# A start tile's load in halves on two queues with an earlier turning, and bn_stats of the up weights in three slots instead of two

## The chip, the cores and the metric

The kernel runs on one core of a Trainium2 chip. The metric is the device time in microseconds (us) of that core, as the median of several executions. Engines are written as in the profile: PE is the matmul engine and PEld its weight loads, DVE the vector engine, ACT the scalar engine, POOL the general-purpose engine, SP the sync engine. SPq and ACTq are the sequencers of SP and ACT, and they issue the loads. A load is issued when its sequencer hands it to the DMA engines, and it has landed when all its data have arrived.

## The reference

```python
def _A_ref(x, wqkv, w_phi, wo):          # x: 1 x 2048 x 512, H = 32 heads of 16
    q, k, v = (x @ wqkv) split into heads
    pq, pk = q @ w_phi, k @ w_phi        # per head
    phi_q = concat(softmax(pq), softmax(-pq));  phi_k likewise
    kv = phi_k^T v;  z = sum over s of phi_k
    return (phi_q kv / (phi_q z + 1e-6)) @ wo

def _B_ref(x, w_gate, w_up, w_down):     # F = 1792
    return ((x @ w_gate) * (x @ w_up)) @ w_down

xn = layernorm(x)
return x + _A_ref(xn, ...) + _B_ref(xn, ...)
```

Everything is bf16. (The code above is condensed from the reference; `setup_inputs` is left out.)

## The kernel before

A small scheduler in the kernel records each instruction with what it reads and writes, and places it on its engine. Between `sc.pin = True` and `sc.pin = False` the order of recording is kept. The parts that matter here are these.

The loads of the start. A tile of x is 128 tokens of 512 numbers, 128 KB; a slice of the v weights is 128 KB too. `SP` and `ACT` name the engine whose sequencer issues the load; SP is the default.

```python
    sc.pin = True
    load_x(0, 1)
    load_x(1, 1, ACT)
    load_v(SP, 0)
    load_v(ACT, 1)
    load_x(2, 1)
    load_v(ACT, 3)
    load_v(SP, 2)
    load_x(3, 1)
    load_gu(SP, 0, (1,))          # first slice of the up weights, 256 KB
    act(sbf("lnv", 0, 1), eps_f, ["eps"], ["pace"])
    load_gu(ACT, 0, (0,))         # first slice of the gate weights, 256 KB
    # ... (later loads cut)
```

The centring of a tile: ACT sums one half of the columns, DVE the other, then DVE subtracts the mean.

```python
    def ln_mean_split(t):
        act(xn_tile(t)[:, 256:], x_tile(t)[:, 256:], [("x", t)], [("mu", t)], scale=1.0 / 512.0,
            accum=mu[:, t:t + 1])
        dve(lambda e: e.tensor_scalar(out=xn_tile(t)[:, :256], in0=x_tile(t)[:, :256], scalar1=1.0 / 512.0,
                                      scalar2=0.0, op0=ALU.mult, op1=ALU.add, accum_out=mua[:, t:t + 1]),
            [("x", t)], [("mua", t)], 256)
```

The pinned start. `warm` is a matmul of constants, `x_transpose` turns half a tile on PE (2 transposes) and copies it back on ACT or DVE, `v_matmul(t, b, qs)` multiplies tile t with the v weights qs.

```python
    warm(7)
    warm(1, 512, [("x", 0)])
    sc.pin = True
    ln_mean_split(0)
    ln_mean_split(1)
    # ... (centring of tiles 0 and 1, turning of tile 0 and of half of tile 1 cut)
    ln_mean_split(2)
    x_transpose(1, 5, 1, DVE)
    warm(1, 128)
    ln_center_whole(2)
    for t in range(2):
        v_matmul(t, t, ((0, 1),), stop=False)
    for t in range(2):
        v_matmul(t, t, ((3,),), start=False, stop=False)
    x_transpose(2, 6, 0)
    x_transpose(2, 4, 1, DVE)
    for t in range(2):
        v_matmul(t, t, ((2,),), start=False)
    # ... (tile 3, then the first gate and up matmuls, which need the first gate and up slices)
```

The statistics of the up weights, 14 `bn_stats` of 128 x 512, seven each in the slots t = 5 and t = 6 of a loop over tiles:

```python
        if t in (5, 6):
            moments(range(7 * (t - 5), 7 * (t - 4)), last)
```

## Time and profile before

| | before |
|---|---|
| median of the first 3 runs | 214.51 us (213.98 to 214.95) |
| span of the profiled execution | 212.9 us |
| PE busy | 98% |
| first transpose on PE, last matmul on PE (start) | 4.49 us, 209.98 us |

From the page of the kernel before: PE's line of busy time, and the chain that ended last, by engine.

```profile
PE 208.2 (98%) x1455; PEld 125.3 (59%) x1476; DVE 167.3 (79%) x281; ACT 143.8 (68%) x350; POOL 109.9 (52%) x137
...
PE 96%; DMA 1%; DVE 1%; issue 1%
```

PE is the limit nearly everywhere. A gain can come only from a place where PE stops. I look for stops in the start-to-start distances of matmuls: 216 ns for 512 columns, 109 ns for 256 and 56 ns for 128 are no stop at full clock, and what exceeds them is.

PE's timeline of the kernel before, 5 to 11 us, with groups of like instructions in one line (columns: start us, busy us, engine, line, operation, tiles, shape, count). L474 is the turning of x, L247 a matmul.

```profile
5.58 1.76 PE L247 MATMUL ps<-arena 128*128 128x512 bf16 x6
7.17 0.39 PE L474 MATMUL ps<-arena 128*128 128x128 bf16 x4
7.39 1.56 PE L247 MATMUL ps<-arena 128*128 128x512 bf16 x6
8.84 0.40 PE L474 MATMUL ps<-arena 128*128 128x128 bf16 x4
9.07 2.12 PE L247 MATMUL ps<-arena 128*128 128x256 bf16 x13
```

The reader sees tile 2 turned at 7.17 us, tile 3 at 8.84 us, and the gate matmuls (256 columns) from 9.07 us, with little lost between: 95 ns and 41 ns by the start-to-start distances.

The issues on ACT's queue in the kernel before, from the timeline of 0.7 to 4.8 us (columns: start us, duration us, engine, line, operation, tiles, count). The second line is v weights 1 and v weights 3 together.

```profile
0.81 0.39 ACTq L272 DMA_DIRECT2D arena<-in_A_x_dram  x1
1.23 0.93 ACTq L292 DMA_DIRECT2D arena<-in_A_wqkv_dram  x2
2.23 0.42 ACTq L292 DMA_DIRECT2D arena<-in_B_w_gate_dram  x1
```

One issue of a whole 128-row load takes 0.39 to 0.45 us here, and ACT is free for arithmetic from 2.65 us.

The same kernel in one stretch (columns: stretch and its length in us; busy us and count of PE, PEld, DVE, ACT, POOL; granted clock, mean busy share of the DMA engines, GB/s).

```profile
4.50:5.50 1.00, 1.00 (x10) 0.79 (x11) 0.70 (x3) 0.58 (x2) 0.00 (x0) 1.00 0.87 269
```

The middle of the kernel before has three more stops, of 133, 143 and 102 ns at 55 to 60 us. DVE's timeline there, where L454 applies the layernorm, L668 is bn_stats and L506 the softmax sum (in brackets: idle us before, and what ended it):

```profile
51.11 0.41 DVE L454 TENSOR_SCALAR arena<-arena 128x512 bf16<-128x512 bf16 x1 [2.20 <-DMA arena<-arena]
...
52.36 1.28 DVE L668 BATCH_NORM_STATS2 arena<-arena 128x6 f32<-128x512 bf16 x2
53.55 1.20 DVE L506 TENSOR_REDUCE arena<-arena 128x64 f32<-128x1024 bf16 x1
54.67 0.68 DVE L894 TENSOR_TENSOR arena<-ps,arena 128x512 bf16<-128x512 f32 x1
```

Two bn_stats stand between the apply and the softmax sum, and the gate multiply (L894), which PE needs, comes after.

PE's timeline of the kernel before, from which the stops can be read: four of the turning at 56.28 and again at 60.24 us, with 16 matmuls between, which at 216 ns would take 3.46 us and with the turning 3.68 us.

```profile
56.28 0.39 PE L381 MATMUL ps<-arena 128*128 128x128 bf16 x4
56.51 3.79 PE L247 MATMUL ps<-arena 128*128 128x512 bf16 x16
60.24 0.40 PE L381 MATMUL ps<-arena 128*128 128x128 bf16 x4
```

It took 3.96 us from turning to turning: the stops of 143 and 102 ns are in it.

### The profile page before, as it was taken

To read this page: it belongs to the slowest core of one execution; us is meant where nothing else is said; L and a number is where in the kernel's file an instruction comes from. 1 tells how busy PE (TensorE), PEld (TensorE's weight loads), DVE (VectorE), ACT (ScalarE), POOL (GpSimd) and SP (SyncE) were. 2 spreads that over 40 slices of the span, in tenths; PEclk is the share of its full clock that TensorE was granted. 3 is DMA by queue.
4 is the path that set the end of the run, shared out by engine and by line. 5 is a ranking of instruction groups with operands and counts; after the bars stand their busy time and mean duration, and the time that the engine had idled before them with its cause. 6 is when DMAs were issued, how large, how long until landed. Compare 5 with 4: busy or idle time off the path is not lost.

```text
span 212.9 us, 4028 instructions
## 1 busy us (share of the span) xinstructions
PE 208.2 (98%) x1455; PEld 125.3 (59%) x1476; DVE 167.3 (79%) x281; ACT 143.8 (68%) x350; POOL 109.9 (52%) x137
## 2 busy tenths in 40 slices
PE   8999999999999999999999999999999999999995
PEld 3575444444444444444444444546888898899884
DVE  4687999985995656578699988996888898898622
ACT  5479899975789999987778977664544444432220
POOL 4031554540311355999995882004549559558540
PEclk9999999999999999999999999999999999999999
DMA  5999780899100030322721340413374646537611
GB/s 163 309 300 375 134 207 0 122 345 147 30 3 0 20 78 3 52 51 49 77 45 29 65 86 0 118 53 52 45 83 125 162 85 154 134 91 175 123 49 49
DMA packets 49251, 22.29 MB, mean 105 GB/s; under 512 B 38096, under 2 KB 47696, under 8 KB 49232
## 3 DMA queue, kind: packets, MB, share of 16 engines
q1 hardware_dynamic: 48272, 21.39, 46.0%
q10 hardware_dynamic: 960, 0.66, 1.0%
q8 instruction: 11, 0.18, 0.4%
q14 instruction: 8, 0.07, 0.2%
HBM read 11.03 MB, written 2.10 MB: 62 GB/s over the span
## 4 chain that ended last, share of the span: by engine, by line
PE 96%; DMA 1%; DVE 1%; issue 1%
PE ps L247 91%; PE ps L611 2%; PE ps L553 2%; DMA arena<-in_A_x_dram 1%; PE ps L381 1%; PE ps L474 1%; DVE arena L427 0%; DVE arena L924 0%; DVE arena L434 0%; PE ps L1001 0%
## 5 line engine op out<-in xcount | busy, mean ns | idle before, releaser
L247 PE MATMUL ps<-arena 128*128 128x512 bf16 (+2 forms) x1139 | 198.4, 329 | 1.1
L247 PEld LDWEIGHTS ps<-arena 128*128 128x128 bf16 (+1 forms) x1160 | 110.7, 98 | 73.8 <-ACT arena L228 1.2
L228 ACT ACTIVATE arena<-ps 128x512 bf16<-128x512 f32 (+3 forms) x117 | 58.6, 539 | 12.9 <-PE ps L247 7.0
L228 ACT ACTIVATE arena<-arena 128x32 f32<-128x32 f32 (+9 forms) x131 | 52.9, 423 | 11.3 <-DVE arena L506 7.2
L894 DVE TENSOR_TENSOR arena<-ps,arena 128x512 f16<-128x512 f32 (+1 forms) x56 | 38.2, 683 | 11.8 <-PE ps L247 6.1
L516 POOL TENSOR_TENSOR arena<-arena 128x1024 bf16<-128x1024 bf16 x16 | 31.8, 1995 | 26.8 <-ACT arena L228 26.8
L506 DVE TENSOR_REDUCE arena<-arena 128x64 f32<-128x1024 bf16 x32 | 38.2, 1210 | 7.6 <-ACT arena L228 7.5
L228 ACT ACTIVATE arena<-ps,arena 128x512 bf16<-128x512 f32 (+1 forms) x55 | 35.9, 672 | 10.9 <-PE ps L247 10.4
L855 POOL TENSOR_TENSOR arena<-arena 128x256 f16<-128x256 f16 x32 | 23.8, 755 | 14.3 <-DMA arena<-arena 13.2
L833 DVE TENSOR_TENSOR arena<-arena 128x896 f16<-128x896 f16 x32 | 26.0, 812 | 3.4 <-PE ps L247 3.4
L228 ACT ACTIVATE ps<-ps 128x256 f32<-128x256 f32 x24 | 8.8, 368 | 29.0 <-PE ps L247 27.0
L924 DVE SCALAR_TENSOR_TENSOR arena<-ps,arena 128x256 bf16<-128x256 f32 (+1 forms) x24 | 13.2, 565 | 8.9 <-PE ps L247 8.7
L773 POOL TENSOR_TENSOR arena<-arena 128x512 f16<-128x512 bf16 x14 | 16.3, 1175 | 5.7 <-DVE arena L894 5.2
L959 POOL TENSOR_TENSOR arena<-arena 128x512 f32<-128x512 f32 x8 | 9.5, 1190 | 17.0 <-ACT arena L228 17.0
L522 POOL TENSOR_TENSOR arena<-arena 128x512 bf16<-128x512 bf16 x16 | 17.0, 1060 | 0.8
L621 DVE TENSOR_TENSOR arena<-ps,arena 128x512 f16<-128x512 f32 x16 | 11.0, 686 | 1.3 <-ACT arena L228 0.5
L405 DVE BATCH_NORM_STATS2 arena<-arena 128x6 f32<-128x512 bf16 x16 | 10.4, 668 | 0.4 <-DMA arena<-in_A_x_dram 0.4
L520 POOL TENSOR_TENSOR arena<-arena 128x32 f32<-128x32 f32 x16 | 5.2, 326 | 10.4 <-ACT arena L228 5.8
L452 POOL TENSOR_SCALAR arena<-arena 128x1 f32<-128x1 f32 x12 | 3.2, 282 | 12.3 <-ACT arena L228 12.3
L668 DVE BATCH_NORM_STATS2 arena<-arena 128x6 f32<-128x512 bf16 x14 | 8.9, 680 | 0.0
L553 PEld LDWEIGHTS ps<-arena 128*128 128x128 bf16 x128 | 6.1, 97 | 3.5
L454 DVE TENSOR_SCALAR arena<-arena 128x512 bf16<-128x512 bf16 x12 | 5.4, 484 | 2.8 <-DMA arena<-arena 2.6
(54 smaller groups left out, 72.9 us busy)
## 6 DMA issues: line engine op xcount, KB each, us to landing
arena<-in_A_x_dram SPq DMA_DIRECT2D x8, 256.0 KB, 3.3
out_dram<-arena SPq DMA_DIRECT2D x15, 128.0 KB, 2.1
arena<-in_B_w_down_dram SPq DMA_DIRECT2D x1, 1792.0 KB, 10.1
arena<-in_A_x_dram SPq DMA_DIRECT2D x3, 512.0 KB, 4.4
arena<-arena SPq DMA_TRANSPOSE x44, 3.1
arena<-in_B_w_gate_dram SPq DMA_DIRECT2D x1, 640.0 KB, 8.7
arena<-in_B_w_up_dram SPq DMA_DIRECT2D x1, 640.0 KB, 9.9
arena<-in_B_w_gate_dram SPq DMA_DIRECT2D x1, 512.0 KB, 5.1
```

The lines of the kernel that those rows point to most:

```text
L228: return sc.step(ACT, lambda e: e.activation(out=out_ap, in_=in_ap, func=func, scale=scale, **kw), reads, writes, 130.0 + 0.833 * n)
L247: ins = e.matmul(out_ap, lhsT=l, rhs=r, start=start and i == 0, stop=stop and i == npair - 1, **kw)
L405: dve(lambda e: e.bn_stats(stats_v[:, t, 0:6], x_tile(t)), [("x", t)], [("st", t)], 512)
L506: dve(lambda e: e.tensor_reduce(out=sm, in_=e_v, axis=AX.X, op=ALU.add), [(name, s, 0), (name, s, 1)], [("sums", sr)], 1024)
L516: pool(lambda e: e.tensor_tensor(out=e_w, in0=e_w, in1=r_w, op=ALU.mult), [(name, s, 0), (name, s, 1), ("rs", n)], [(name, s, 0), (name, s ...
L522: pool(lambda e: e.tensor_tensor(out=e_v[:, :, 1, :], in0=e_v[:, :, 1, :], in1=rat[:, :, None].to_broadcast([128, H, 16]), op=ALU.mult), [ ...
L621: dve(lambda e: e.tensor_tensor(out=o_tile(t).rearrange("p (b h f) -> p b h f", b=2, f=16), in0=nd[:, :, :, 0:16], in1=w_v[:, r].unsqueeze ...
L773: pool(lambda e, ft=ft: e.tensor_tensor(out=hH_v[:, ft, 0:512], in0=hT_v[:, ft, 0:512], in1=r2w, op=ALU.mult), [("hT", ft, 0), "r2w", ("x" ...
L833: dve(lambda e, k=k, i0=i0, i1=i1, op=op: e.tensor_tensor(out=s_block(p, k), in0=i0, in1=i1, op=op), ks + more, [s_key(p, k)] + over.get(k ...
L855: pool(lambda e, k=k, i0=i0, i1=i1, op=op: e.tensor_tensor(out=so_block(p, k), in0=i0, in1=i1, op=op), ks + [("so", p, m) for m in more], ...
L894: dve(lambda e: e.tensor_tensor(out=h_v[:, ft, sg * 512:(sg + 1) * 512], in0=bank(bu), in1=g, op=ALU.mult), [("ps", bu), ("g", s)] + ([("j ...
L924: dve(lambda e: e.scalar_tensor_tensor(out=o, in0=src, scalar=inv, in1=resid, op0=ALU.mult, op1=ALU.add), keys + [rkey, "inv"], [("ostg", ...
```

## The change

Its intent: (a) tile 2 comes sooner, as two halves of 64 rows, 64 KB each, one on each queue; (b) so it can be centred and turned sooner, and PE turns it one matmul earlier; (c) the bn_stats stand five, five and four to a slot, so that fewer are ahead of the softmax sum, for which the gate multiplies wait.

```diff
@@ loads
+    def load_x_half(t, h, eng):
+        p = slice(h * 64, h * 64 + 64)
+        o, i = x_tile(t)[p, :], rows(x_flat, t, 1)[p, 0, :]
+        sc.dma(eng, lambda e: e.dma_start(o, i), [], [("x", t) if h else ("x", t, 0)], 65536)
...
     load_v(ACT, 1)
-    load_x(2, 1)
+    load_x_half(2, 0, SP)
+    load_x_half(2, 1, ACT)
     load_v(ACT, 3)
@@ ln_mean_split
+        xs_k = [("x", t)] + [("x", t, 0)] * (t == 2)
-        ... [("x", t)] ...            (twice, as what the two sums read)
+        ... xs_k ...
@@ the pinned start
     ln_mean_split(2)
+    ln_center_whole(2)
     x_transpose(1, 5, 1, DVE)
     warm(1, 128)
-    ln_center_whole(2)
     for t in range(2):
         v_matmul(t, t, ((0, 1),), stop=False)
-    for t in range(2):
-        v_matmul(t, t, ((3,),), start=False, stop=False)
+    v_matmul(0, 0, ((3,),), start=False, stop=False)
     x_transpose(2, 6, 0)
     x_transpose(2, 4, 1, DVE)
-    for t in range(2):
-        v_matmul(t, t, ((2,),), start=False)
+    v_matmul(0, 0, ((2,),), start=False)
+    v_matmul(1, 1, ((3,), (2,)), start=False)
@@ scales
-        if t in (5, 6):
-            moments(range(7 * (t - 5), 7 * (t - 4)), last)
+        if 5 <= t < 8:
+            moments(range(5 * (t - 5), min(NF, 5 * (t - 4))), last)
```

More of the change, by code (lines that the diff above doesn't have):

```diff
@@ L424, in ln_mean_split @@
     def ln_mean_split(t):
-        act(xn_tile(t)[:, 256:], x_tile(t)[:, 256:], [("x", t)], [("mu", t)], scale=1.0 / 512.0,
+        xs_k = [("x", t)] + [("x", t, 0)] * (t == 2)
+        act(xn_tile(t)[:, 256:], x_tile(t)[:, 256:], xs_k, [("mu", t)], scale=1.0 / 512.0,
             accum=mu[:, t:t + 1])
@@ L428, in ln_mean_split @@
                                       scalar2=0.0, op0=ALU.mult, op1=ALU.add, accum_out=mua[:, t:t + 1]),
-            [("x", t)], [("mua", t)], 256)
+            xs_k, [("mua", t)], 256)
     def ln_center_split(t):
```

## The prediction

> **What bounds the kernel.** The page gives a span of 212.9 us with PE busy 98%; the chain that ended last is 96% PE, after 2.6 us of the first x load. TensorE is the limit from its first real instruction (4.49 us) on; DVE (79%), ACT (68%) and DMA matter only where PE stops for them. I looked for such stops in the timeline of PE, where 216 ns from start to start (512 columns), 109 (256) and 56 (128) are no stop:
>
> - Until about 6.2 us the distance is 427 ns, half speed. The Trainium skill, "TensorE: Matmul & The Clock Gate" (the HAM clock gate), says the first ~3.4 us of activity run at half clock, on a free-running window; the trace agrees with 427 and 216 ns. The change touches nothing on PE before 6.2 us.
> - 7.9 us: 95 ns for ACT's copy of turned tile 2; 8.8 us: 41 ns for DVE's centring of tile 3.
> - 55.4 us: 133 ns and 58.4 us: 143 ns for gate multiplies on DVE behind bn_stats; 60.2 us: 102 ns for ACT's exponentials, ACT being busy without pause from 54.8 us, when DVE's softmax sum freed it.
> - Single distances of twice the usual, every 9 us, are missing records.
>
> So the change can win about 0.14 + 0.38 = 0.5 us at most, 0.24%.
>
> **What the change does.**
> 1. Tile 2 (128 KB) lands at 5.67 us, beside v weights 3 (5.85). In halves on two queues it comes ahead of them: my estimate is 5.1-5.3 us, v weights 3 at 6.3, still before PE wants them (6.7). The extra ACT issue (0.43 us) ends near 3.1 us, before the first activation at 3.41. ACT's mean of tile 2 starts at 5.69 and cannot start before ACT's two copies end at 5.58, so only 0.1 us of that comes through; centring ahead of tile 1's copy saves as much again. PE turns tile 2 one 216 ns matmul earlier, so its copy is ready 0.2 us sooner: the 95 ns stop goes, the 41 ns stop stays or shrinks (tile 3's load lands at 7.41). Gain 0.05-0.14 us, best guess 0.1.
> 2. The bn_stats (0.67 us each, 0.60 apart) stay 14, but one leaves the queue ahead of the softmax sum at 53.56 us. Sum and gate multiply come up to 0.6 us sooner; the stops at 55.4 and 58.4 go. ACT's squares wait for the multiply and its gate copy for PE, so ACT moves only 0.15 us; the stop at 60.2 stays or grows. Gain 0.1-0.38 us, best guess 0.2.
> 3. Four bn_stats move to 61-65 us. The cast for the norms comes 1.3 us later than 65.0, PE takes it at 69.6, and DVE idles 1.7 us at 66.6: no cost.
>
> Engines keep their busy times within 0.3 us.
>
> **Prediction.** 214.2 us, 0.3 below 214.51; three runs of before alone spread over 1 us. Range 213.5 to 214.9. Faster by over 2%: 0.01; within 2%: 0.98; slower: 0.01.
>
> **What would show it.** Right: tile 2 lands before 5.4 us; PE's distances near 7.9 and at 55-59 us are 216 ns; ACT's wait near 54.8 us ends sooner; PE from first transpose to last matmul takes 0.2-0.5 us less. Wrong: tile 2 no sooner, v weights 3 late so that PE stops at 6.7 us, or new stops of PE at 61-70 us.
>
> **What would make it wrong.** Later landing of v weights 3 or of the first gate slice, the reordered ACT queue near 61 us (placing v now waits behind a DVE sum), or noise larger than the effect.

## The result, and the profile after

| | before | after |
|---|---|---|
| median (range) of 4 runs each, same chip | 214.43 us (213.98 to 214.95) | 214.86 us (214.70 to 214.93) |
| ratio, 95% interval | | 1.0018 (0.9995 to 1.0042) |
| span of the profiled execution | 212.9 us | 213.2 us |
| first transpose, last matmul (start) | 4.49, 209.98 us | 4.72, 210.25 us |

A ratio here and below is the mean time of one kernel's runs over the mean of the other's of the same rounds, so it is not quite the ratio of the medians. The time lies in the predicted range. The direction that the prediction gave, 0.3 us less, did not come: the 10 runs of the changed kernel have a mean of 214.97 us and none is under 214.70, while the 54 runs of the kernel before have a mean of 214.32 us and 46 of them are under 214.70. That is 0.65 us more, by means over several batches.

The page of the kernel after: PE's busy line and the chain by engine.

```profile
PE 209.1 (98%) x1476; PEld 125.7 (59%) x1476; DVE 167.5 (79%) x281; ACT 144.2 (68%) x350; POOL 110.7 (52%) x137
...
PE 94%; DMA 3%; ACTq 1%; DVE 0%; ACT 0%; issue 0%
```

(PE's count and busy time differ because some 20 records of matmuls are missing in the trace of before; both kernels issue the same number.) The chain now holds 3% of DMA and 1% of ACT's sequencer. The chain of the kernel after from 3 to 12 us, in order of time (columns: start us, us, what; the piece that began before 3 us is shown whole), tells which:

```profile
2.34 0.83 ACTq L297
...
3.23 6.48 DMA arena<-in_B_w_gate_dram
9.71 0.05 issue
9.76 2.35 PE ps L247 x16
```

ACT's sequencer took 0.83 us to issue v weights 3, the load of the first gate slice was issued only after it, at 3.23 us, and took 6.48 us; PE waited for it. The issues on ACT's queue after the change:

```profile
1.25 0.45 ACTq L297 DMA_DIRECT2D arena<-in_A_wqkv_dram  x1
1.73 0.57 ACTq L277 DMA_DIRECT2D arena<-in_A_x_dram  x1
2.34 0.83 ACTq L297 DMA_DIRECT2D arena<-in_A_wqkv_dram  x1
3.23 0.42 ACTq L297 DMA_DIRECT2D arena<-in_B_w_gate_dram  x1
```

The half load takes 0.57 us to issue, not 0.43, although it is half as large, and the whole load behind it takes 0.83 us. The gate slice is issued 1.00 us later than before (3.23 instead of 2.23), and ACT is kept until 3.65 us. So its first mean starts at 3.70 us instead of 3.41, and PE's first transpose at 4.72 instead of 4.49. ACT's first mean before:

```profile
3.41 0.42 ACT L228 ACTIVATE arena<-arena 128x256 bf16<-128x256 bf16 x1 [0.99 <-DMA arena<-in_A_x_dram]
```

The first means of DVE and ACT after:

```profile
3.49 0.42 DVE L434 TENSOR_SCALAR_CACHE_REDUCE arena<-arena 128x256 bf16<-128x256 bf16 x1 [0.23 <-DMA arena<-in_A_x_dram]
3.70 0.42 ACT L228 ACTIVATE arena<-arena 128x256 bf16<-128x256 bf16 x1 [0.28 <-DMA arena<-in_A_x_dram]
```

Both need tile 0, which landed at 3.38 us before and 3.47 us after. DVE began with it; ACT, which was still issuing, began 0.21 us later, and the rest of its 0.29 us is tile 0's landing. A late tile 0 alone does as much: in the profiles of stats_only, turn_and_stats and extra_64rows (told of below), where ACT had issued its loads in time, tile 0 landed at 3.62 to 3.70 us, and the first transpose started at 4.73 to 4.81 us.

The DMA engines in the same stretch as before:

```profile
4.50:5.50 1.00, 0.78 (x8) 0.57 (x8) 0.94 (x4) 0.45 (x4) 0.00 (x0) 1.00 0.38 119
```

They were busy for a share of 0.38 only in a microsecond in which the kernel before moved 269 GB/s. Counted from the transfers in the trace, 1.19 MB had come by 7 us instead of 1.39.

PE's timeline after, and PE's waits over the whole span (columns: waited for; us in total, times, longest us):

```profile
5.81 1.80 PE L247 MATMUL ps<-arena 128*128 128x512 bf16 x5
7.45 0.38 PE L481 MATMUL ps<-arena 128*128 128x128 bf16 x4
7.67 1.67 PE L247 MATMUL ps<-arena 128*128 128x512 bf16 x7
9.18 0.39 PE L481 MATMUL ps<-arena 128*128 128x128 bf16 x4
9.76 1.48 PE L247 MATMUL ps<-arena 128*128 128x256 bf16 x10 [0.19 <-DMA arena<-in_B_w_gate_dram]
```

```profile
PE ps L1008 <- PEq L1386: 0.8, 1, 0.8
PE ps L481 <- DVE arena L441: 0.3, 1, 0.3
PE ps L247 <- DMA arena<-in_B_w_gate_dram: 0.2, 1, 0.2
```

Tile 2 is turned at 7.45 us, later than before, though the turning stands one matmul earlier. By start-to-start distances PE loses 240 ns at 6.8 us, until v weights 3 have landed (7.09 us), and 355 ns at 9.3 us, until the first gate slice has (9.71 us; the wait listed is shorter because the modelled end of the matmul before it hides a part). Together with the 0.23 us at the first transpose, and less the 0.14 us of small stops that went, that makes some 0.7 us more in the first 10 us.

The middle, on DVE, looks as the prediction wanted it (line numbers are shifted by 7):

```profile
50.69 0.41 DVE L461 TENSOR_SCALAR arena<-arena 128x512 bf16<-128x512 bf16 x1 [1.08 <-DMA arena<-arena]
...
51.94 0.69 DVE L675 BATCH_NORM_STATS2 arena<-arena 128x6 f32<-128x512 bf16 x1
52.54 1.20 DVE L513 TENSOR_REDUCE arena<-arena 128x64 f32<-128x1024 bf16 x1
```

One bn_stats fewer stands ahead of the sum, which comes 1.85 us after the apply instead of 2.44 us, and PE's three stops of 0.38 us are gone. In this pair of profiles the balance is therefore 0.7 us lost, 0.38 us won, 0.3 us worse, which is what the starts of the last matmul say (210.25 less 209.98). Whether the 0.38 us was won by the change is the question of the second group of experiments.

Landing times of the start, read from the trace (us from the start of the span), for the two kernels and for each once more from the experiments:

| | tile 2 | v weights 3 | v weights 2 | tile 3 | first gate slice | first up slice |
|---|---|---|---|---|---|---|
| before | 5.67 | 5.85 | 6.28 | 7.41 | 7.33 | 8.25 |
| before, second profile | 7.00 | 7.21 | 7.62 | 8.28 | 8.70 | 9.61 |
| after | 5.31 and 5.53 | 7.09 | 6.81 | 7.54 | 9.71 | 10.09 |
| after, second profile | 5.19 and 5.82 | 7.61 | 6.23 | 7.79 | 9.69 | 9.89 |

### The profile page after: what moved, and what is told of

The parts are those of the page before. It is cut to its first block, busy times and chain, and to the rows that moved or that the text cites. A ratio compares the mean times of both kernels' runs of the same rounds, so it can differ in the third digit from the quotient of the medians. Undisturbed runs are those within 1.5% of the kernel's fastest.

```text
span 213.2 us, 4052 instructions
## 1 busy us (share of the span) xinstructions
PE 209.1 (98%) x1476; PEld 125.7 (59%) x1476; DVE 167.5 (79%) x281; ACT 144.2 (68%) x350; POOL 110.7 (52%) x137
## 4 chain that ended last, share of the span: by engine, by line
PE 94%; DMA 3%; ACTq 1%; DVE 0%; ACT 0%; issue 0%
PE ps L247 90%; DMA arena<-in_B_w_gate_dram 3%; PE ps L560 2%; PE ps L618 2%; PE ps L387 1%; ACTq L297 1%; ACTq L277 0%; DVE arena L931 0%; ACT L1201 0%; ACT arena L228 0%
## 5 line engine op out<-in xcount | busy, mean ns | idle before, releaser
L560 PEld LDWEIGHTS ps<-arena 128*128 128x128 bf16 x128 | 6.1, 97 | 3.5
L618 PEld LDWEIGHTS ps<-arena 128*128 128x128 bf16 x128 | 6.2, 97 | 1.2
```

Source lines behind the costliest of these rows:

```text
L618: ins = e.matmul(bank(b0 + c // 4, (c % 4) * CW, CW), lhsT=ph[:, c, :], rhs=kvz_v[:, c, :], start=True, stop=True)
```

## The experiments

Two questions stood. On the loads: the theory was that the half loads cost time by themselves, by their slow issue and by what that delays; the rivals were that the earlier turning or the statistics did it, or that the first microseconds simply vary that much. On the statistics: the theory was that the three slots take PE's stops at 55 to 60 us away; the rival was that those stops belonged to the one execution that had been profiled. All 12 kernels gave correct outputs.

| kernel | median (range) of 6 runs, us | before's median, same batch | ratio (95% interval) |
|---|---|---|---|
| stats_only | 214.52 (213.86 to 214.98) | 214.07 | 1.0007 (0.9981 to 1.0033) |
| loads_turn_only | 215.04 (214.80 to 215.57) | 214.07 | 1.0035 (1.0012 to 1.0058) |
| turn_and_stats | 214.50 (213.98 to 214.92) | 214.07 | 1.0005 (0.9980 to 1.0031) |
| halves_both_sp | 214.79 (214.67 to 215.07) | 214.07 | 1.0022 (0.9998 to 1.0047) |
| before_again | 214.52 (214.01 to 215.17) | 214.11 | 1.0004 (0.9980 to 1.0029) |
| after_again | 215.08 (214.70 to 215.31) | 214.11 | 1.0033 (1.0012 to 1.0053) |
| extra_64rows | 214.59 (214.08 to 215.64) | 214.11 | 1.0016 (0.9988 to 1.0044) |
| halves_by_column | 214.59 (214.43 to 214.82) | 214.11 | 1.0012 (0.9992 to 1.0032) |
| v01_in_one | 214.11 (213.72 to 214.41) | 214.23 | 0.9990 (0.9976 to 1.0004) |
| x23_in_one | 214.74 (214.36 to 215.04) | 214.23 | 1.0019 (1.0004 to 1.0034) |
| v01_x23_in_one | 214.21 (214.14 to 214.61) | 214.23 | 1.0001 (0.9988 to 1.0013) |
| v01_old_stats | 214.38 (213.78 to 215.14) | 214.03 | 1.0011 (0.9986 to 1.0035) |

Kernels of one batch stand together (four batches: the first four, the next four, the next three, the last). The batch with before_again is the measure of what may be believed: the same kernel against itself gave 1.0004, with an interval of a quarter of a per cent to either side.

### The change taken apart: stats_only, loads_turn_only, turn_and_stats

stats_only is the kernel before with part (c) alone:

```diff
-        if t in (5, 6):
-            moments(range(7 * (t - 5), 7 * (t - 4)), last)
+        if 5 <= t < 8:
+            moments(range(5 * (t - 5), min(NF, 5 * (t - 4))), last)
```

> The kernel before with bn_stats in slots of 5, 5 and 4 and nothing else. Theory A (the bn_stats slots win, the half loads lose): 0.38 us faster than before, about 214.05 us, ratio 0.998; the stops of PE of 133, 143 and 102 ns at 55.4, 58.4 and 60.2 us are gone, the first 10 us are as before. Rival B (the middle stops went only because PE arrived later after a later start, so that the stats part wins nothing by itself): same time as before, stops of 0.2 us or more remain between 55 and 61 us.

It was measured at 1.0007 times before, a null within the noise. The interval reaches down to 0.9981: a gain of 0.2 us (0.1%) lies well inside it, and the hoped-for 0.38 us (0.18%) just inside, so the number alone excludes neither; no gain showed.

loads_turn_only is the change without part (c), so 7 and 7 again:

```diff
-        if 5 <= t < 8:
-            moments(range(5 * (t - 5), min(NF, 5 * (t - 4))), last)
+        if t in (5, 6):
+            moments(range(7 * (t - 5), 7 * (t - 4)), last)
```

> The change without its bn_stats part. Theory A: 0.6 to 0.7 us slower than before, about 215.1 us; the first transpose at about 4.72 us, a stop of 240 ns at 7.0 us for v weights 3 and of 350 ns at 9.4 us for the first gate slice, and the three stops at 55 to 61 us still there or shrunk by what the start lost. Rival (the late landings of the run after are chance): within 0.2 us of before.

It was measured at 1.0035 (1.0012 to 1.0058), 0.75 us by that ratio, and not one of its 6 runs is under 214.80. Its trace repeats what the kernel after showed: issues of 0.55 and 0.85 us on ACT's queue, the first transpose at 4.73 us, v weights 3 at 7.26 us, the first gate slice at 9.67 us. PE's wait in its profile:

```profile
PE ps L247 <- DMA arena<-in_A_wqkv_dram: 0.6, 1, 0.6
```

So parts (a) and (b) make the time worse, and by about as much as the whole change does. The three stops at 55 to 60 us are not in its profile.

turn_and_stats is the change with tile 2 loaded whole on SP, as before, so parts (b) and (c) (cut: the line of `ln_mean_split` that goes with it):

```diff
-    load_x_half(2, 0, SP)
-    load_x_half(2, 1, ACT)
+    load_x(2, 1)
```

> The change with tile 2 loaded whole on SP as before, the earlier turning and the bn_stats kept. Theory A: 0.4 to 0.5 us faster than before, about 213.95 us, a little below stats_only; landings as before (tile 2 at 5.7, v weights 3 at 5.9, first gate slice at 7.3 us), no stop of 95 ns at 7.9 us. Rival D (the earlier turning makes PE wait, not the loads): slower than stats_only by 0.2 us or more, with stops at 7.0 us.

It was measured at 1.0005. The gain of 0.4 to 0.5 us that the theory gave did not come. In the same batch its mean is 214.45 us, that of stats_only 214.49 us and that of loads_turn_only 215.09 us. The earlier turning thus costs nothing that shows beside stats_only, and with (c) no effect that shows, the halves are left as the part that costs. The direct comparison, the whole change against the change without halves, is across batches: 1.0033 (after_again, below) against 1.0005. Its profile isn't a pretty one: tile 2 landed at 6.60 us there, and PE stood 554 ns for it at 6.9 us. The earlier turning thus makes PE lean on an early tile 2, which the whole load doesn't always give.

### How much of it is the chance of the start: before_again and after_again

These are the two kernels, unchanged, run again as if they were experiments.

> The kernel before once more, as a null test and a second profile. Ratio 1.000 within 0.003. If the three stops of PE at 55 to 61 us (378 ns in all) belong to the kernel, they are there again with 0.3 to 0.4 us; if they come of the late landing of a transposing DMA at 51.0 us in that one execution (49.8 to 51.1 us in the other profiles), they are smaller or gone. First loads: 1.3 to 1.4 MB moved by 7 us.

before_again gave 1.0004. Its one profiled execution was among the slower ones of this kernel (215.17 us), with tile 2 at 7.00 us and v weights 3 at 7.21 us, 1.3 to 1.4 us later than in the first profile of the very same kernel. PE's wait there:

```profile
PE ps L247 <- DMA arena<-in_A_wqkv_dram: 0.8, 1, 0.8
```

So the landings of the start vary by more than a microsecond from one execution to the next, and a late v weights 3 costs the kernel before as much as it costs the changed one. None of the three stops at 55 to 60 us is in this profile.

> The changed kernel once more, on the chip of the others of this call. If the half loads cost time: ratio 1.002 to 1.004 over before, 1.2 MB moved by 7 us (before: 1.4), v weights 3 at 7.0 us or later, first gate slice at 9.5 us or later. If the first result was chance: ratio within 0.001 of 1 and landings as before.

after_again gave 1.0033 (1.0012 to 1.0053), so the changed kernel costs time, and the 1.0018 of the first measurement, whose interval reached just below 1, fits that. Its profile has the same two late landings, v weights 3 at 7.61 us and the first gate slice at 9.69 us:

```profile
PE ps L247 <- DMA arena<-in_A_wqkv_dram: 1.0, 1, 1.0
```

By then PE had lost so much that the late gate slice cost nothing more. In all three profiles with halves of 64 rows on both queues the v weights 3 landed at 7.1 to 7.6 us and the gate slice at 9.7 us. The kernel before had 5.85 and 7.33 us in one profile and 7.21 and 8.70 us in its other. What is chance for the kernel before is the rule for the changed one.

### Shape or number of the loads: halves_by_column, halves_both_sp, extra_64rows

halves_by_column keeps the number of loads, their bytes and their queues, and only cuts the tile the other way, 128 rows of 512 bytes each instead of 64 rows of 1 KB:

```diff
-        p = slice(h * 64, h * 64 + 64)
-        o, i = x_tile(t)[p, :], rows(x_flat, t, 1)[p, 0, :]
+        c = slice(h * 256, h * 256 + 256)
+        o, i = x_tile(t)[:, c], rows(x_flat, t, 1)[:, 0, c]
```

> The change with tile 2 halved by columns, 128 rows of 512 B on each queue, in place of 64 rows of 1 KB. Theory F (loads of 64 rows are what is slow: issues of 0.57 us in place of 0.43 us, and the next one too): issues back at 0.43 us, 1.3 to 1.4 MB by 7 us, time 0.3 to 0.7 us below after_again. Rival A1 (the count of loads is what costs, whatever their shape): issues and landings as in after, time within 0.2 us of after_again.

Its issues on ACT's queue:

```profile
1.73 0.45 ACTq L277 DMA_DIRECT2D arena<-in_A_x_dram  x1
2.21 0.45 ACTq L297 DMA_DIRECT2D arena<-in_A_wqkv_dram  x1
2.73 0.42 ACTq L297 DMA_DIRECT2D arena<-in_B_w_gate_dram  x1
```

Each is back at 0.45 us or less, the gate slice is issued at 2.73 us instead of 3.23, and the first transpose starts at 4.51 us. The mean time is 214.62 us, against 215.06 us of after_again in the same batch; the ranges of the six runs each overlap by 0.12 us only. So the slow issue belongs to the 64-row shape, or at least to what was cut, not to the number of loads, and some 0.4 us of the cost goes with it. The rest, 0.3 us against before (1.0012, not clear of noise), has a likely reason, which no run isolates: one more load stands ahead of the gate slice on ACT's queue, and it landed at 9.42 us in this profile (7.33 and 8.70 us in the two of before), tile 3 at 7.92 us. PE stood for tile 3 there:

```profile
PE ps L481 <- DVE arena L446: 0.5, 1, 0.5
```

halves_both_sp puts both halves of 64 rows on SP's queue:

```diff
     load_x_half(2, 0, SP)
-    load_x_half(2, 1, ACT)
+    load_x_half(2, 1, SP)
```

> The change with both halves of tile 2 on the SP queue, so that ACT issues what it issued before. Theory A1 (a half load costs about as much issue time, 0.5 us, as a whole one, on whichever queue it stands): first transpose back at 4.5 us and first gate slice back near 7.3 us, but v weights 2, tile 3 and the first up slice land 0.5 to 1 us later than before and PE stops for them: 0.1 to 0.6 us slower than turn_and_stats. Rival C (only the ACT queue hurts, because ACT also computes): within 0.1 us of turn_and_stats.

ACT's queue is as before here; tile 0 landed at 3.40 us, ACT's first mean starts with DVE's at 3.42 us and the first transpose at 4.50 us. In the three profiles with halves on both queues ACT began at 3.70 us, 0.11 to 0.21 us after DVE. So part of the delay at the first transpose is ACT's issuing, and the rest the landing of tile 0. The two halves take 1.20 us to issue on SP together. The second half lands at 6.57 us, and PE stands 697 ns for tile 2. It was measured at 1.0022, its interval just reaching 1. So this way round the halves probably cost too, by another wait.

extra_64rows is the kernel before with one more, unread load of 64 rows to a spare buffer, on ACT's queue at the place of the change's half (cut: the allocation of the buffer):

```diff
     load_x(2, 1)
+    sc.dma(ACT, lambda e: e.dma_start(sb("spare", 0, 512)[0:64, :], rows(x_flat, 2, 1)[0:64, 0, 0:512]),
+           [], ["spare"], 65536, is_out=True)
     load_v(ACT, 3)
```

> The kernel before with one more load on the ACT queue, in the place where the change has its half: 64 rows of 1 KB into a spare buffer that nothing reads. Theory A1 (a further half load holds up the ACT queue, whatever it loads): issues after it on ACT 0.5 to 1 us later, v weights 3 at 6.7 us or later, first gate slice at 8.7 us or later, time 0.2 to 0.6 us above before. Rival E (only its 64 KB count, 0.2 us at 300 GB/s): landings 0.2 us later, time within 0.2 us of before.

It was issued in 0.54 us and the load behind it in 0.59 us, not 0.83, and the gate slice at 2.96 us. The time was 1.0016, with runs from 214.08 to 215.64 us; no cost is shown, and one no larger than the interval isn't excluded. One half load on one queue is therefore not the whole of it: the 0.83 to 0.86 us for the load behind a half came only where both queues had halves. It isn't shown why. A long issue is not peculiar to halves, though: later on SP's queue, whole loads of 128 rows took up to 0.88 us where no half had been issued (the second up slice at 3.24 us in v01_x23_in_one, below). That more loads under way slow the issue is a rival that no run isolates.

### Fewer loads instead of more: v01_in_one, x23_in_one, v01_x23_in_one

If more loads cost, fewer may win. v01_in_one keeps the earlier turning and the three slots, loads v weights 0 and 1 as one load of 256 KB on SP, and tile 2 whole on ACT in the place that this frees (cut: the body of `load_v01` and the line of `ln_mean_split`):

```diff
-    load_v(SP, 0)
-    load_v(ACT, 1)
-    load_x_half(2, 0, SP)
-    load_x_half(2, 1, ACT)
+    load_v01(SP)            # wv_v[:, 0:2, :] from 256 rows of the weights
+    load_x(2, 1, ACT)
```

> Tile 2 brought forward without one more load: v weights 0 and 1 are one load of 256 KB on SP, and tile 2 goes whole on ACT in the place of v weights 1; earlier turning and bn_stats as in the change. Theory G (at the start PE waits for bytes in the order of their landing, and fewer, whole loads land sooner than more, smaller ones): tile 2 lands at 4.6 to 5.2 us, v weights 3 by 6.2 us, first gate slice by 8.5 us, time 0.2 to 0.6 us below before (about 213.9 us on average). Rival (the first loads cannot be improved by order; whatever is brought forward holds up something else by as much): v weights 0 and 1 land after 5.6 us and hold up PE, time within 0.15 us of before.

It was measured at 0.9990 (0.9976 to 1.0004), the best: 0.4% under the changed kernel by the two ratios (0.9990 and 1.0033), and against before not clear of noise: its mean is 0.19 us lower, at the edge of the 0.2 to 0.6 us. Tile 2 landed at 5.16 us, v weights 3 at 6.02 us, the gate slice at 7.31 us. The DMA engines in the stretch in which they were least busy after the change:

```profile
4.50:5.50 1.00, 1.00 (x10) 0.80 (x11) 0.71 (x3) 0.57 (x3) 0.00 (x0) 1.00 1.01 335
```

Tile 2 comes here earlier than the halves brought it, with one load fewer than before, and 1.50 MB had come by 7 us. PE's one wait in its profile is the one at 0.8 us, for its own start.

x23_in_one is the kernel before with tiles 2 and 3 as one load (128 rows of 2 KB), and tile 2 turned after the matmuls with v weights 2:

```diff
-    load_x(2, 1)
+    load_x(2, 2)
     load_v(ACT, 3)
     load_v(SP, 2)
-    load_x(3, 1)
...
-    x_transpose(2, 6, 0)
-    x_transpose(2, 4, 1, DVE)
     for t in range(2):
         v_matmul(t, t, ((2,),), start=False)
+    x_transpose(2, 6, 0)
+    x_transpose(2, 4, 1, DVE)
```

> The kernel before with tiles 2 and 3 as one load of 128 rows of 2 KB on SP, tile 2 turned after the matmuls of v weights 2, bn_stats as before (7 and 7). Theory G: tile 3 lands 0.8 us or more sooner, PE has no stop for its centring, the 90 to 180 ns stops near 7.9 and 8.8 us go; time 0 to 0.4 us below before, with fewer executions above 214.5 us. Rival: tile 2 later by 0.6 us holds up PE at 7.6 us as much as is won, time within 0.15 us of before.

It was measured at 1.0019 (1.0004 to 1.0034), a small loss. Tile 2 with tile 3 behind it lands at 6.51 us only, v weights 3 at 6.70 and v weights 2 at 7.05 us; PE stops for them. A merged load is a gain only if nothing in it is wanted early.

v01_x23_in_one does both, with tiles 2 and 3 as one load on ACT's queue (shown against v01_in_one):

```diff
-    load_x(2, 1, ACT)
+    load_x(2, 2, ACT)
...
-    load_x(3, 1)
```

> Both: v weights 0 and 1 as one load on SP, tiles 2 and 3 as one load on ACT in the place of v weights 1, two loads fewer than before; earlier turning and bn_stats as in the change. Theory G: tiles 2 and 3 land by 5.8 us, v weights 2 and 3 by 6.6 us, first gate and up slices by 8.5 us; 1.4 MB or more by 7 us; time 0.3 to 0.8 us below before. Rival: v weights 0 and 1 after 5.8 us hold up PE, time within 0.2 us of before.

It was measured at 1.0001, not the 0.3 to 0.8 us below before, so the second merge gained nothing.

### The statistics once more: v01_old_stats

This is v01_in_one with 7 and 7 again. Its start is an early one, so if the stops at 55 to 60 us come from the two slots, they must be there.

```diff
-        if 5 <= t < 8:
-            moments(range(5 * (t - 5), min(NF, 5 * (t - 4))), last)
+        if t in (5, 6):
+            moments(range(7 * (t - 5), 7 * (t - 4)), last)
```

> v01_in_one with bn_stats back in two slots of 7. With the earliest start so far (last matmul at 209.4 us), the gate multiplies behind bn_stats have the least slack. Theory A (the slots of 5, 5 and 4 win 0.2 to 0.4 us once PE is early): the stops at 55 to 61 us are back, 0.2 to 0.4 us in all, ratio near 1.000. Rival B (the stops belonged to one execution with a late transposing DMA): no stops over 30 ns between 20 and 200 us, ratio near 0.999 as for v01_in_one.

By time it is 1.0011, beside 0.9990 of v01_in_one in another batch, with overlapping intervals: undecided. Its profile decides more. PE and DVE of v01_old_stats in the stretch that was shown of before:

```profile
55.81 0.39 PE L389 MATMUL ps<-arena 128*128 128x128 bf16 x4
56.03 3.62 PE L247 MATMUL ps<-arena 128*128 128x512 bf16 x16
59.49 0.39 PE L389 MATMUL ps<-arena 128*128 128x128 bf16 x4
```

```profile
49.20 0.41 DVE L463 TENSOR_SCALAR arena<-arena 128x512 bf16<-128x512 bf16 x1 [0.62 <-DMA arena<-arena]
...
50.45 1.28 DVE L677 BATCH_NORM_STATS2 arena<-arena 128x6 f32<-128x512 bf16 x2
51.65 1.20 DVE L515 TENSOR_REDUCE arena<-arena 128x64 f32<-128x1024 bf16 x1
```

From turning to turning it takes 3.68 us, no stop, with the same two bn_stats ahead of the sum. DVE begins 1.91 us earlier than in the first profile of before (49.20 against 51.11 us), mostly because the apply waited 0.62 us for the transposing DMA instead of 2.20 us, while PE is only 0.47 us earlier (55.81 against 56.28 us). Of the six profiles with 7 and 7 only the first of before has the stops; before_again, loads_turn_only, extra_64rows, x23_in_one and this one have none. The rival held: those stops belonged to one execution, in which a transposing DMA landed late. A late landing alone isn't enough. In loads_turn_only the apply came at 51.02 us, nearly as late as the 51.11 us of before, and DVE's softmax sum at 53.47 us; but PE, held up at the start, came to the turning at 56.79 instead of 56.28 us, and did not stop. What made the DMA land late wasn't found, and what the three slots are worth when it does and PE is early stays open.

## Why the prediction was right and wrong

The number was right, 214.2 us with a range of 213.5 to 214.9. The bound on the gain was right too: PE busy 98%, and no more than half a microsecond of stops to win. It didn't bound a loss, and that the measured 214.86 us fell inside the range was luck: it lies 0.04 us below the upper end, and the median of after_again, 215.08 us, lies above it. The two reasoned terms both failed, and the sign with them. Some of the signs that were to show the prediction right came true all the same (PE's distances near 7.9 and at 55 to 59 us are 216 ns), but PE from the first transpose to the last matmul took 205.53 us instead of 205.49, not 0.2 to 0.5 us less: the loss lay at the first transpose, at v weights 3 and at the first gate slice.

- **"Tile 2 lands ... my estimate is 5.1-5.3 us."** Nearly so: 5.31 and 5.53, 5.19 and 5.82, 4.91 and 5.20 us in the three profiles. The second half missed the prediction's own sign of "before 5.4 us" in two of three. It bought nothing, since everything else in front of the turning came later.
- **"The extra ACT issue (0.43 us) ends near 3.1 us, before the first activation at 3.41."** This is the step that failed first. It counted a half load as one more load of the usual 0.43 us. The half took 0.57 us and the load behind it 0.83 us, so ACT issued until 3.65 us, its first mean started 0.29 us late (3.70 instead of 3.41; 0.21 us of it by the issuing), and the first transpose 0.23 us late. "The change touches nothing on PE before 6.2 us" fell with it. The Trainium skill, "DMA: Bandwidth & Descriptors", section "Issuing engines are not separate DMA queues", says that several issuing engines save only sequencer time, which is usually small relative to the DMA itself. It was smaller here too, 0.83 us against 4.75 us from issue to landing for v weights 3, but it counted, as ACT's arithmetic and the next load waited for it.
- **"v weights 3 at 6.3, still before PE wants them (6.7)."** They landed at 7.1 to 7.6 us in the three profiles, and PE stopped 240 to 1210 ns for them. The prediction's text had this as a sign of being wrong, and it came.
- **The first gate slice** was named among what could go wrong, but not costed. It landed at 9.7 us instead of 7.33 (8.70 in the second profile of before), and PE stopped up to 355 ns for it. The same skill page, section "Rules for kernel authors", advises on "Two transfers to disjoint partition halves": "Don't bother — they serialize", and to use one 128-partition transfer. The runs agree with the advice and go further: it cost 0.33 to 0.35% in after_again and loads_turn_only, while the whole load in turn_and_stats showed no cost (1.0005).
- **"The 95 ns stop goes, the 41 ns stop stays or shrinks ... best guess 0.1."** Both went, but the start as a whole lost about 0.7 us in the profile, and the whole kernel 0.65 us by the pooled means. In place of a gain of 0.1 us came a loss six to seven times as large.
- **"The stops at 55.4 and 58.4 go. ... Gain 0.1-0.38 us, best guess 0.2."** On DVE it happened as costed, the sum came 0.59 us sooner after the apply (1.85 instead of 2.44 us). But in five of six profiles with the old slots PE doesn't stop there at all. The step that failed was to take the stops of one profiled execution for a property of the kernel. The term showed no gain: 1.0007 (0.9981 to 1.0033), an interval that leaves room for the 0.2 us.
- **"The cast for the norms comes 1.3 us later than 65.0 ... no cost."** No cost was right; the cast came 0.2 us later only (65.2 us).
- **The clock of the start.** The prediction cited the Trainium skill, "TensorE: Matmul & The Clock Gate", section "Part 1: The HAM clock gate", for a half clock of about 3.4 us on a free-running window. The traces agree that it varies: the half-speed distances (427 ns for 512 columns, 107 for 128) ended between about 4.9 and 6.5 us in the profiles where they could still be seen, and before the first transpose, at 4.5 to 4.8 us, in others. In the first profile of before that is some 5.4 us after PE's first matmul (6.2 less 0.82), not 3.4. The end varies among kernels with and without halves, so it adds to the noise; with one or two profiles of a kernel it isn't shown to explain any difference.

What is shown: half loads of 64 rows on both queues cost this kernel about 0.3% (1.0018, 1.0033 and 1.0035 in three measurements), and with a whole load in their place no cost shows; the issue of such loads is slower, and ACT's arithmetic and the later loads start later for it. What stays open: why the DMA engines carried only 119 GB/s at 4.5 to 5.5 us (171 and 215 in the other two profiles with halves on both queues, 269 and 220 in the two of before, but 212 in turn_and_stats too, with a whole load), why the first gate slice took 6.48 us from issue to landing after the change, as in the second profile of before (6.47), but 5.10 us in the first, and why the load behind a half is slow on ACT's queue only if SP's queue has a half as well. The traces record no more of the queues than issue and landing.

## What to carry to other kernels

When a load is split, cost the issue of every piece and of the load behind it, on the engine that issues, and list what lands later, not only what lands sooner; here one whole load fewer brought the tile as early as the halves did, and left the rest on time. Before a stop of PE is counted as something to win, look for it in a second profile of the same kernel. And where the first microseconds vary by more than the effect, a repeated null test tells what a difference of 0.2% is worth.

## What the Trainium skill lacked or had wrong

- "DMA: Bandwidth & Descriptors" calls the time to initiate a DMA usually small relative to the DMA itself and gives no figure by shape for SP and ACT. The runs show 0.39 to 0.48 us for a whole 128-row load in the first 2.3 us, 0.54 to 0.6 us for one of 64 rows, 0.57 to 0.59 us for the load behind it, and 0.83 to 0.86 us for that load on ACT's queue when both queues had halves. Whole loads of tiles and weight slices issued later on SP's queue took 0.43 to 0.88 us.
- The same page's rule on disjoint partition halves says that they don't help. It doesn't say that they can cost: 1.0033 and 1.0035 here, against 1.0005 with the whole load.
- No page tells how much landings vary between executions of one kernel: tile 2 landed at 5.67 and 7.00 us, v weights 3 at 5.85 and 7.21 us, in two profiles of the kernel before.
- "TensorE: Matmul & The Clock Gate" puts the end of the slow clock at about 4 us with half a microsecond to either side. Counted from PE's first matmul at 0.82 us, it came here between less than 4 and about 5.7 us. The same section gives a wider spread elsewhere, 6, 11 or 14 slow matmuls for one kernel, which fits these traces better: by estimate, 4 and 5.7 us are 9 and 13 distances of 427 ns. And the profile's clock column shows 1.00 in stretches in which the distance is still 427 ns.
